# An adaLN transformer block on one core: 57 of 108 quad products moved to GpSimd in four pieces each, 3+3 quad buffers, two-bank exponential groups to the end

## The chip, the cores and the metric

The kernel runs on one core of one Trainium2 chip. The engines are TensorE (PE, with its weight loads shown as PEld), VectorE (DVE), ScalarE (ACT), GpSimd (POOL) and SyncE (SP), which issues the DMAs. The metric is the device time of one execution in microseconds. Before the change it is 815.04 us, the median of 3 runs from 815.03 to 815.05 us.

## The reference

One block over 2048 rows of 640 columns, 32 heads of 20 columns, in bf16. Only `A_x` is used as input; `B_x` is not.

```
mod = (silu(c) @ w_mod).reshape(1, 6, 1, 640)
sa, ca, ga, sb, cb, gb = mod[:, 0..5]
h = layernorm(x) * (1 + ca) + sa
q, k, v = split(h @ wqkv)                       # 32 heads of 20
o = softmax(q @ k.T / sqrt(20)) @ v             # per head, 2048 x 2048 scores
x = x + ga * (o @ wo)
h = layernorm(x) * (1 + cb) + sb
x = x + gb * (((h @ w_gate) * (h @ w_up)) @ w_down)    # F = 1536
```

The scores are 32 x 2048 x 2048 values, and each needs an exponential. That is the bulk of the elementwise work.

## The kernel before

**A planner in the builder.** The kernel file holds a small scheduler (`Sched`): every instruction is a `Task` with an engine, a planned duration, dependencies and a priority. The scheduler runs through planned time and fixes, for each engine, the order of its instructions. `emit_program` writes these orders out as five instruction streams with semaphore waits. So the chip runs a fixed order on each engine, in which every instruction waits for what it needs.

**Units of attention.** Queries go through in five chunks of 512, 512, 512, 256 and 256 rows (`CHUNKS`). An item is one chunk with four heads; there are 8 items in a chunk, 40 in all. The scores of an item are cut into units of 128 keys-partitions x 512 columns: 64 units in an item of a 512-row chunk, 32 in one of a 256-row chunk, 2048 in all. PE computes a unit's scores into one PSUM bank. The scores are scaled so that they count in 1/128 of a power of two.

**Two ways to the exponential.** Most units go to ScalarE: a group of two units (banks 0 and 1 or 3 and 4), or of three (banks 0 to 2), is exponentiated by one ACTIVATE (line 1484) into a slot of a ring `PP`, four slots for even groups and four for odd ones. From group 580 on (`HEADG`) even groups have three banks; up to there bank 2 serves as a third bank of the pool `G`, which holds projections, FFN results and quads' scores. The other units go to VectorE, four at a time; four such units are a quad (`QUADS` gives the number of quads of each item). A quad costs:

- four evacuations P1 (line 1508): PSUM bank to an int16 buffer `DB`, 128x512 each;
- two splits of that buffer, 128x2048 int16: M (line 1540, the mantissa, into a slot of `DSS`) and EX (line 1548, the exponent, into another slot);
- one product X (line 1545): `DB` times the mantissa term, 128x2048 bf16, in place in the slot of M.

Both terms are then multiplied with the values, so a quad's units pass through the value matmuls (line 2005) twice (`NTERM` = 2), a ScalarE unit once. There are `NB0` = 2 buffers `DB` and `NSS` = 3 slots `DSS`.

**Value products.** Line 2005 accumulates an item's output, with the softmax denominator in an extra value column, in the one bank 7. When all units of an item are in, VectorE transposes the bank (T1, line 1632), takes the reciprocal of the denominators, GpSimd multiplies (T3, line 1638), VectorE transposes back (T4, line 1646), and DMAs copy the heads to where the output projection reads them. The next item's value products wait for T1.

**Work beside it.** During chunk 0 PE computes the projections to queries, keys and values (lines 1107, 1171, 911). During each chunk from the second on it does the suffix of the chunk before: output projection, layer norm, gate, up and down projections (line 911 and, in the tail, 907), with evacuations on VectorE. `GATE_F` spreads these over the groups of the chunk. The suffix of the last chunk is the tail. Where PE would idle, it may run matmuls that add zeros (lines 2355 and 2357).

**PE's order.** `pick_pe` prefers a group's score step, to which up to two units of quads may be attached (`d_attach`), if their banks in `G` are free. After that come value products and then projection or FFN rounds. `STAGE` overrides the thresholds of these choices item by item.

**The shared port in the planner.** Tasks that the planner takes to use the SBUF port pair which VectorE and GpSimd share carry `lk`: splits and products on VectorE (1), most GpSimd tasks (1). `Sched.locked` keeps such a task from starting while one of the other engine runs. Pieces of a product on GpSimd carry `lk` = 2: before, they may not start either while VectorE has a port task ready. `Sched.lock` also makes such a piece wait for VectorE's last port task. With `X_POOL` = 0 no product goes to GpSimd, so no task has `lk` = 2 before the change.

Of the kernel before, what the change touches and what calls it, by code (L numbers as in the profile page):

```python
# [30 lines left out]
HAM_MIN = 2550.0  # L31

# [85 lines left out]
class Sched:  # L118
# [32 lines left out]
    def locked(self, eng, task):  # L151
        if not task.lk:
            return False
        if self.lk_end["pool" if eng == "dve" else "dve"] > self.t:
            return True
        if task.lk == 2:
            for d in self.readyl["dve"]:
                if d.lk and d.rt <= self.t and d.gate <= self.progress and (d.cond is None or d.cond()) and all(
                        a[0].avail() is not None and a[0].avail()[0] <= self.t for a in d.acq):
                    return True  # L160
        return False
# [160 lines left out]
def emit_program(nc, sched, nsem_dma=56):  # L322
# [83 lines left out]
    with nc.Block() as block:  # L406
# [20 lines left out]
        def _(e):  # L427
# [5 lines left out]
QUADS = ((0, 4, 3, 3, 3, 3, 4, 4),  # L433
         (3, 4, 2, 4, 3, 4, 4, 4),
         (3, 3, 4, 4, 3, 4, 4, 4),
         (1, 2, 1, 2, 2, 1, 1, 2),
         (1, 1, 1, 1, 1, 1, 1, 1))
D_LEAD = 0.451
NB0, NSS = 2, 3
HEADG = 580  # L440
# [7 lines left out]
X_POOL, X_PIECES, POOL_NS = 0, 4, 1.95  # L448
X_LAST = 2
X_TAIL = 0  # L450
XBACK = 1
HOLD = 110
PVTOL = 249
XDPRIO = 1.447
# [8 lines left out]
WM_GATE = 9  # L463
# [9 lines left out]
PVMIN, PVMAX, PVCAP = 2, 7, 13  # L473
# [13 lines left out]
GATE_F = (0.468, 0.693, 0.969, 0.732, 1.0)  # L487
FILL_MIN = 4153.722
# [23 lines left out]
    0: {"X_LATE": -179.96, "D_RES": 74, "EAGER": 9, "PVMAX": 14},  # L512
    1: {"HOLD": 91, "D_LATE": 10, "PVMAX": 7},
    2: {"DL": 0.376, "D_LATE": 17},
    3: {"STEAL_GAP": 200, "PVMAX": 5, "FILL_MIN": 4781.051, "X_LATE": 38.763},
    5: {"EAGER": 7, "D_RES": 27, "PVCAP": 8},
    6: {"PVCAP": 12, "FILL_MIN": 4102.43, "D_LATE": 12, "PVMIN": 2},
    7: {"DL": 0.501, "PVCAP": 8, "PVTOL": 347},
    10: {"PVMAX": 8, "X_LATE": -27.967, "EAGER": 11, "D_LATE": 9},
    11: {"EAGER": 11, "DL": 0.443, "X_LATE": -8.435, "FILL_MIN": 4364.854, "PVTOL": 245, "HOLD": 134, "PVMAX": 9, "PVCAP": 13},  # L520
    12: {"FILL_MIN": 4969.105, "D_LATE": 7, "STEAL_GAP": 194.93, "X_LATE": -138.337, "DL": 0.459},
    13: {"DL": 0.417, "D_RES": 10, "HOLD": 84, "PVMAX": 6},
    14: {"D_LATE": 14, "D_RES": 22, "FILL_MIN": 4272.896, "EAGER": 10, "X_LATE": -52.696, "STEAL_GAP": 200},
    15: {"X_LATE": -15.741, "FILL_MIN": 4338.164, "HOLD": 175, "EAGER": 13},
    16: {"FILL_MIN": 3909.78, "D_RES": 55, "HOLD": 133, "PVCAP": 11},
    17: {"DL": 0.465, "D_LATE": 17, "PVMAX": 9, "PVMIN": 2, "STEAL_GAP": 195.663},
    18: {"FILL_MIN": 4326.704, "D_RES": 10},
    19: {"D_LATE": 18, "DL": 0.471, "FILL_MIN": 3976.707},
    20: {"DL": 0.391, "D_LATE": 14, "PVCAP": 13, "FILL_MIN": 5000},
    21: {"D_RES": 10, "PVCAP": 20, "HOLD": 96, "PVMAX": 6, "PVMIN": 2, "D_LATE": 19},  # L530
    22: {"PVMAX": 7, "FILL_MIN": 3913.503, "D_RES": 17, "X_LATE": -76.434, "EAGER": 6, "D_LATE": 16, "PVCAP": 13},
    23: {"PVTOL": 247, "PVMAX": 7, "D_RES": 23},
    24: {"PVCAP": 13, "PVMAX": 7, "PVMIN": 2, "FILL_MIN": 4085.526, "DL": 0.464, "EAGER": 7, "STEAL_GAP": 200, "HOLD": 231},
    25: {"HOLD": 174, "X_LATE": 22.894, "D_RES": 13, "FILL_MIN": 4068.834, "DL": 0.608, "PVCAP": 17, "D_LATE": 14, "EAGER": 5, "Z_LATE": -10.124, "PVTOL": 224},
    26: {"D_RES": 21, "X_LATE": -37.237, "PVMAX": 9, "PVCAP": 13, "STEAL_GAP": 193.843, "DL": 0.411, "FILL_MIN": 3349.471, "D_LATE": 18},
# [1897 lines left out]
```

## Time and profile before

| what | value |
|---|---|
| median of 3 runs | 815.04 us (815.03 to 815.05) |
| the profiled execution | 815.03 us |
| its span, first to last instruction | 813.2 us |
| granted TensorE clock, mean | 1.000 |
| exponentials on ScalarE: of two banks, of three | 676, 97 in the grouped rows (774 in all) |
| first and last exponential | 16.0 us to 779.4 us |
| GpSimd's normalizing products of 128x512 (T3) | 24, mean 1526 ns; shortest 1.05 us, longest 4.85 us |
| DMA moved | 54.70 MB, mean 67 GB/s |

The span is the time between the first and the last instruction in the trace; some 1.8 us of the execution lie outside it. An instruction's duration on ScalarE and VectorE overlaps that of the next, so rates are taken from starts or from busy time. A row of the grouped view names the line, the engine, the operation, output and inputs, the count, the busy time and the mean of one, then the idle time of the engine in front of these instructions and what ended it. A row of the waits names who waited for whom: total, times, longest. A row of a stretch lists the busy time of PE, PEld, DVE, ACT and POOL in it.

### The profile page before, as it was taken

Reading aid. Unit: us, or ns where it says so; the run is one execution under the profiler, and the core shown is the slowest. Engines: PE = TensorE matmul, PEld = TensorE weight load, DVE = VectorE, ACT = ScalarE, POOL = GpSimd, SP = SyncE. Lnnn points to the kernel's source line nnn. Section 1 sums busy time; section 2 is a strip of 40 time slices with the busy share of each in tenths; the row PEclk is TensorE's granted clock in tenths of the full one; section 3 lists DMA queues with packets and bytes.
Section 4 is the critical chain, followed back from the end, with each engine's and each line's share of the span. In section 5 each row is a group of like instructions: output and inputs, shape, how many; then the busy total and the mean of one; then the engine's idle time right before and its main releaser. Section 6 shows DMA issues by size and latency. Waiting matters only on the chain.

```text
span 813.2 us, 28869 instructions
## 1 busy us (share of the span) xinstructions
PE 785.0 (97%) x12485; PEld 305.5 (38%) x12485; DVE 724.7 (89%) x1283; ACT 772.8 (95%) x816; POOL 79.4 (10%) x106
## 2 busy tenths in 40 slices
PE   9999999999999999999999999999888999999998
PEld 4433333322233223233233322333244444454567
DVE  7989999899999999999999999998999878667763
ACT  7899999999999999999999999999999999999941
POOL 3300000020002000000011000000021000001000
PEclk9999999999999999999999999999999999999999
DMA  9624211114330244000400222000400145106520
GB/s 305 210 86 106 68 46 38 50 30 126 93 67 25 52 107 130 23 11 22 93 6 6 55 54 55 6 19 23 87 8 15 45 95 129 45 22 128 126 61 17
DMA packets 116445, 54.70 MB, mean 67 GB/s; under 512 B 83916, under 2 KB 116320, under 8 KB 116320
## 3 DMA queue, kind: packets, MB, share of 16 engines
q1 hardware_dynamic: 115391, 51.72, 24.7%
q8 instruction: 99, 1.62, 0.8%
q10 hardware_dynamic: 928, 1.15, 0.4%
q14 instruction: 27, 0.21, 0.1%
HBM read 41.85 MB, written 8.41 MB: 62 GB/s over the span
## 4 chain that ended last, share of the span: by engine, by line
PE 47%; ACT 34%; DVE 12%; issue 6%; POOL 0%; DVEq 0%; ACTq 0%; POOLq 0%
ACT PP L1484 34%; PE ps_all L911 16%; PE ps_all L1448 14%; PE ps_all L2005 10%; DVE DB L1508 5%; PE ps_all L907 3%; DVE DSS L1545 2%; DVE DSS L1548 1%; DVE DSS L1540 1%; PE ps_all L1171 1%; PE ps_all L1107 1%; PE ps_all L2355 1%; PE ps_all L1068 1%; DVE wd L1434 1%; DVE OT L1632 1%
## 5 line engine op out<-in xcount | busy, mean ns | idle before, releaser
L1484 ACT ACTIVATE PP<-ps_all 128x1024 bf16<-128x1024 f32 (+1 forms) x774 | 754.2, 1168 | 5.0 <-PE ps_all L1448 3.0
L1448 PE MATMUL ps_all<-QT,KT 32*128 32x512 bf16 (+1 forms) x2560 | 308.4, 340 | 17.9 <-ACT PP L1484 11.6
L1508 DVE TENSOR_SCALAR DB<-ps_all 128x512 int16<-128x512 f32 x404 | 267.4, 680 | 33.7 <-PE ps_all L1448 32.5
L1448 PEld LDWEIGHTS ps_all<-QT,KT 32*128 32x128 bf16 x2560 | 81.5, 91 | 262.5 <-ACT PP L1484 227.6
L2005 PE MATMUL ps_all<-PP,Vf 128*32 128x512 bf16 (+2 forms) x2076 | 163.5, 343 | 0.0
L1545 DVE TENSOR_TENSOR DSS<-DB,DSS 128x2048 bf16<-128x2048 bf16 x101 | 123.6, 1223 | 0.0
L911 PE MATMUL ps_all<-h2T,stg 128*32 128x512 bf16 (+1 forms) x1744 | 116.4, 344 | 1.8 <-DVE DB L1508 1.1
L1638 POOL TENSOR_TENSOR OTn<-OT,invT 128x512 bf16<-128x512 f32 (+1 forms) x39 | 46.7, 1197 | 601.0 <-DVE invT L1636 601.0
L2005 PEld LDWEIGHTS ps_all<-PP,Vf 128*32 128x32 bf16 (+1 forms) x2076 | 46.9, 94 | 85.5 <-issue 78.7
L2005 PE MATMUL ps_all<-DSS,Vf 128*32 128x512 bf16 (+1 forms) x968 | 77.9, 348 | 0.9 <-DVE DSS L1545 0.5
L1540 DVE TENSOR_SCALAR DSS<-DB 128x2048 int16<-128x2048 int16 x101 | 71.1, 704 | 0.8
L1548 DVE TENSOR_SCALAR DSS<-DB 128x2048 int16<-128x2048 int16 x101 | 69.7, 690 | 0.3 <-PE ps_all L2005 0.3
L911 PE MATMUL ps_all<-wd,hprod 128*32 128x320 bf16 (+1 forms) x1312 | 58.9, 284 | 0.5 <-DVE xckt L1730 0.2
L911 PEld LDWEIGHTS ps_all<-h2T,stg 128*32 128x32 bf16 x1744 | 38.9, 95 | 36.6 <-issue 18.3
L911 PEld LDWEIGHTS ps_all<-wd,hprod 128*32 128x32 bf16 x1312 | 30.8, 96 | 17.9 <-issue 8.0
L2005 PEld LDWEIGHTS ps_all<-DSS,Vf 128*32 128x32 bf16 x968 | 24.3, 95 | 24.5 <-issue 15.0
L911 PE MATMUL ps_all<-wV,hT 128*32 128x320 bf16 (+1 forms) x704 | 32.3, 289 | 0.1
L1171 PE MATMUL ps_all<-hT,wq 128*32 128x512 bf16 x375 | 31.6, 382 | 0.1
L911 PE MATMUL ps_all<-wo,Ocp 128*32 128x320 bf16 (+1 forms) x632 | 28.9, 286 | 1.1 <-DVE DB L1508 0.6
L1863 DVE TENSOR_TENSOR hprod<-ps_all,gsb 128x512 bf16<-128x512 f32 x36 | 24.4, 678 | 3.3 <-PE ps_all L911 3.3
L1632 DVE STREAM_TRANSPOSE OT<-ps_all 128x512 f32<-128x512 f32 (+1 forms) x40 | 24.1, 602 | 2.5 <-PE ps_all L2005 2.3
L2357 PE MATMUL ps_all<-ident 128*32 128x512 bf16 x284 | 25.7, 384 | 0.3 <-DVE DB L1508 0.2
(125 smaller groups left out, 505.5 us busy)
## 6 DMA issues: line engine op xcount, KB each, us to landing
stg<-in_B_w_gate_dram SPq DMA_DIRECT2D x50, 160.0 KB, 2.6
stg<-in_B_w_up_dram SPq DMA_DIRECT2D x50, 160.0 KB, 2.4
QT<-q_rows SPq DMA_DIRECT2D x22, 128.0 KB, 2.0
KT<-k_rows SPq DMA_DIRECT2D x84, 32.0 KB, 1.8
wm<-in_w_mod_dram SPq DMA_DIRECT2D x3, 800.0 KB, 5.6
x<-in_A_x_dram SPq DMA_DIRECT2D x7, 320.0 KB
xck<-in_A_x_dram SPq DMA_DIRECT2D x3, 640.0 KB
wd<-in_B_w_down_dram SPq DMA_DIRECT2D x1, 1920.0 KB
```

The costliest lines, as they stand in the source:

```text
L911: return lambda e, b: e.matmul(ps[32 * x:32 * x + 32, b, c0 + o:c0 + o + w], lhs()[:, 32 * x:32 * x + 32], rhs() if w == n else rhs()[:, o ...
L1171: f = [lambda e, b_, k=k, x=x: e.matmul(ps[x:x + min(32, w - x), b_, :], wx[:, k, r0 + x:r0 + min(x + 32, w)], hT[tc][:, k, :], tile_posit ...
L1448: ems.append(lambda e, i=i, kt=kt: e.matmul(dstf()[:, i * u.n:(i + 1) * u.n], KT[32 * u.s:32 * u.s + 32, u.j, kt * 128:(kt + 1) * 128], QT ...
L1484: return e.activation(PPs[g % 2][:, cellp["p"], 0:nu * 512], ps[:, b0:b0 + nu, :].rearrange("p b c -> p (b c)"), AFT.Exp, scale=ESCALE)
L1508: return e.tensor_scalar(DB0[:, st_["slot"], x * 512:(x + 1) * 512], bank(cell["b"]), EBIAS, 0.0, op0=ALU.add, op1=ALU.max)
L1540: return e.tensor_scalar(DSS[:, st_["ss"][0], :], DB0[:, st_["slot"], :], 0x7F, 0x3F00, op0=ALU.bitwise_and, op1=ALU.bitwise_or)
L1545: return e.tensor_tensor(d, DB0[:, st_["slot"], :].bitcast(BF16), d, ALU.mult)
L1548: return e.tensor_scalar(DSS[:, st_["ss"][1], :], DB0[:, st_["slot"], :], 0x7F80, 2, op0=ALU.bitwise_and, op1=ALU.bitwise_or)
L1632: t1 = Task("dve", n * 1.1 + 70, lambda e: e.transpose(OT[:, 0:n], ps[:, BPV, 0:n].rearrange("p (b q r) -> p b r q", q=32, r=2)), [], prio ...
L1638: f3 = lambda e: e.tensor_tensor(OTn[:, 0:n].rearrange("p (b c r) -> p b r c", c=32, r=2), OT[:, 0:n].rearrange("p (b r c) -> p b r c", c= ...
L2005: ems.append(lambda e, i=i, kt=kt, stt=stt, stp=stp: e.matmul(ps[32 * s:32 * s + mc, BPV, 0:u.n], Vf[:, (kt * H + 4 * u.j + s) * VW:(kt * ...
L2357: task.emits = [lambda e, x=x: e.matmul(ps[32 * x:32 * x + 32, b_, :].rearrange("p (a b) -> p a b", a=4), ident[:, 32 * x:32 * x + 32], id ...
```

## The change

It has six parts.

1. **Products on GpSimd.** `X_POOL` = 1: each quad's product except the last quad's may be done by VectorE as one 128x2048 operation, or by GpSimd as four operations of 128x512 (`X_PIECES`), whichever the planner starts first. In the plan 57 of 108 products go to GpSimd and 51 to VectorE. A piece waits for M and for EX of its quad. The splits get priority 0.75, ahead of P1 (0.8); VectorE's product gets 1.343.
2. **When a piece may start.** With `LKTOL` a piece may start although VectorE has a port task ready, if VectorE's work ahead of that task lasts until at most 300 ns before the piece's end in the plan.
3. **Quads.** 108 in place of 101: per chunk 25, 29, 30, 12, 12 in place of 24, 28, 29, 12, 8. ScalarE's units fall from 1644 to 1616. Which units of an item form its quads is generalized, so that an item may have more quads than one diagonal of heads and key tiles gives.
4. **Buffers.** Three `DB` buffers in place of two, three `DSS` slots as before.
5. **Two-bank groups to the end.** `HEADG` = 1000 is past the last group, so no group has three banks, bank 2 stays with `G`, and all slots of the ring have two banks (which frees the memory of the third `DB` buffer).
6. **Choices of the planner.** New thresholds for each item (`STAGE`), new gates, `WM_GATE` 8 in place of 9 (a load of modulation weights may start one group earlier), and in the tail a projection round that is blocked may be overtaken by any round of higher priority. `XB0`, `XSS` and what uses them are 0 and do nothing.

```diff
-            for d in self.readyl["dve"]:
-                if d.lk and d.rt <= self.t and d.gate <= self.progress and (d.cond is None or d.cond()) and all(
+            tt = max(self.t, self.free_at["dve"])
+            for d in sorted(self.readyl["dve"], key=lambda x: (x.prio, x.seq)):
+                if d.rt <= self.t and d.gate <= self.progress and (d.cond is None or d.cond()) and all(
                         a[0].avail() is not None and a[0].avail()[0] <= self.t for a in d.acq):
-                    return True
+                    if d.lk:
+                        return tt < self.t + task.dur - LKTOL
+                    tt += d.dur
...
-QUADS = ((0, 4, 3, 3, 3, 3, 4, 4),
-         (3, 4, 2, 4, 3, 4, 4, 4),
-         (3, 3, 4, 4, 3, 4, 4, 4),
+QUADS = ((0, 4, 3, 3, 3, 4, 4, 4),
+         (3, 5, 2, 4, 3, 4, 4, 4),
+         (4, 2, 4, 4, 4, 4, 4, 4),
          (1, 2, 1, 2, 2, 1, 1, 2),
-         (1, 1, 1, 1, 1, 1, 1, 1))
+         (0, 2, 1, 1, 3, 0, 3, 2))
-NB0, NSS = 2, 3
-HEADG = 580
+NB0, NSS = 3, 3
+XB0, XSS = 0, 0
+HEADG = 1000
-X_POOL, X_PIECES, POOL_NS = 0, 4, 1.95
-X_LAST = 2
+X_POOL, X_PIECES, POOL_NS = 1, 4, 1.95
+X_LAST = 1
-XBACK = 1
+XBACK = 0
-XDPRIO = 1.447
+XDPRIO = 1.343
-WM_GATE = 9
+WM_GATE = 8
-PVMIN, PVMAX, PVCAP = 2, 7, 13
+PVMIN, PVMAX, PVCAP = 2, 7, 12
-GATE_F = (0.468, 0.693, 0.969, 0.732, 1.0)
-FILL_MIN = 4153.722
+GATE_F = (0.446, 0.693, 0.969, 0.658, 1.0)
+FILL_MIN = 4190.746
...
-                q = kg // 4
-                u.is_d = q < nq and s == kg % 4
+                x4 = nkg // 4
+                q = kg // 4 + x4 * ((s - kg) % 4)
+                u.is_d = q < nq
...
-        for q in quads:
+        for q in sorted(quads, key=lambda q: (q[0].kts[0] // (4 * rr), q[0].s)):
             dquads.append((it, q))
...
-                    if blocked and task.name[:3] != "col":
+                    if blocked and task.name[:3] != "col" and not (pvstate["sidx"] >= NG and task.prio < cand.prio):
                         continue
```

The task of a piece was in the file before and is now reached:

```
t = Task("pool", w * POOL_NS + 180.0, fxp, [tm, te], prio=2.0 + .1 * qi + .01 * x, name=f"XP.{qi}")
t.lk = 2
```

## The prediction

> **What bounds the kernel now.** I read the engine totals first, then ScalarE's waits, then the starts of the exponentials, then busy time by stage.
>
> ```profile
> PE 785.0 (97%) x12485; PEld 305.5 (38%) x12485; DVE 724.7 (89%) x1283; ACT 772.8 (95%) x816; POOL 79.4 (10%) x106
> ```
>
> Three engines are near full and GpSimd is nearly empty, so totals don't name the bound. ScalarE's waits do:
>
> ```profile
> ACT h2Tc L1770 <- PE ps_all L1763: 9.9, 1, 9.9
> ACT gsb L1826 <- PE ps_all L907: 9.3, 12, 1.4
> ACT PP L1484 <- PE ps_all L1448: 3.0, 6, 1.3
> ```
>
> The two large waits lie behind the last exponential (779.4 us). In front of it the exponentials run from 16.0 us almost without a gap; the timeline of ScalarE shows 0.7 us of idle after 61 us. So up to 779.4 us the end is set by the number of units on ScalarE times its price. The starts in three stretches of 100 us (count, durations, first and last start):
>
> ```profile
> L1484 ACT ACTIVATE PP<-ps_all x110: 1017/1132/1252, 99.3 to 199.1; 128x1024 bf16<-128x1024 f32 x110
> L1484 ACT ACTIVATE PP<-ps_all x111: 1019/1154/1323, 199.1 to 300.0; 128x1024 bf16<-128x1024 f32 x111
> L1484 ACT ACTIVATE PP<-ps_all x89: 1017/1451/1613, 649.4 to 749.9; 128x1536 bf16<-128x1536 f32 x45, 128x1024 bf16<-128x1024 f32 x44
> ```
>
> A two-bank group comes every 99.8/109 to 100.9/110, about 0.919 us over the stretches of this stage, so 0.4595 us for a unit of 512 columns. A pair of a three-bank and a two-bank group takes 2 x 100.5/88 = 2.284 us for five units, 0.4568 us for a unit. Durations overlap, so I count starts and not means. The other engines by stage (PE, weight loads, DVE, ACT, POOL):
>
> ```profile
> 260.00:360.00 100.00, 99.30 (x1371) 31.08 (x1374) 97.28 (x159) 99.90 (x109) 6.19 (x5) 1.00 0.25 65
> 320.00:560.00 240.00, 234.33 (x3407) 77.20 (x3404) 235.75 (x380) 239.43 (x261) 19.37 (x18) 1.00 0.14 33
> 680.00:740.00 60.00, 57.59 (x1322) 29.19 (x1314) 43.27 (x80) 59.69 (x53) 4.84 (x7) 1.00 0.26 63
> 779.40:813.20 33.80, 30.59 (x425) 24.52 (x420) 16.18 (x44) 5.53 (x15) 1.10 (x2) 0.99 0.07 23
> ```
>
> From 320 to 560 us DVE is 98% full: no further quad fits there. Late (680 to 740 us) DVE is 72% full, but PE 96%. The tail of 33.8 us is PE's.
>
> **Exponentials removed.** Seven more quads take 28 of 1644 units off ScalarE: 28 x 0.4595 = 12.9 us less. Four quads are in the last chunk, three in the first three.
>
> **Three-bank groups given up.** 484 units ran in pairs of 3+2; as two-bank groups each costs 0.4595 - 0.4568 = 0.0027 us more: 1.3 us (0 by the pair at 600 to 700 us, which took 0.459 a unit). I take 1.3.
>
> **Products moved.** The rows, with count, busy time and mean of one:
>
> ```profile
> L1508 DVE TENSOR_SCALAR DB<-ps_all 128x512 int16<-128x512 f32 x404 | 267.4, 680 | 33.7 <-PE ps_all L1448 32.5
> L1545 DVE TENSOR_TENSOR DSS<-DB,DSS 128x2048 bf16<-128x2048 bf16 x101 | 123.6, 1223 | 0.0
> L1540 DVE TENSOR_SCALAR DSS<-DB 128x2048 int16<-128x2048 int16 x101 | 71.1, 704 | 0.8
> L1548 DVE TENSOR_SCALAR DSS<-DB 128x2048 int16<-128x2048 int16 x101 | 69.7, 690 | 0.3 <-PE ps_all L2005 0.3
> ```
>
> DVE does 108 - 57 = 51 products in place of 101: 50 x 1.223 = 61.2 us less. The seven quads add 28 x 0.662 (267.4/404) = 18.5 and 14 x 0.697 = 9.8 us. DVE goes from 724.7 to about 692 us. GpSimd gets 57 x 4 = 228 pieces of 128x512. No such piece is in the trace; the nearest row is its normalizing product on 128x512 f32, 1.05 us where nothing holds it up, 0.62 us on 256 columns, so a piece is bounded by 0.62 below and by the worst such row, 4.85 us, above. I take 1.05: the same columns, two inputs. That is 239 us on an engine that has 734 us free, off the path by itself. By the Trainium skill (GPSIMD Engine Reference, Performance versus the Vector engine), elementwise work belongs on VectorE, since GpSimd's tensor_tensor on 2048 fp32 elements takes 4497 ns; by that 57 products would be an estimated 256 us, which changes the load and not the bound.
>
> **The price is the lock.** What a piece blocks is shown around 176 us, first GpSimd, then DVE:
>
> ```profile
> 175.93 4.85 POOL L1638 TENSOR_TENSOR OTn<-OT,invT 128x512 bf16<-128x512 f32 x1 [20.39 <-DVE invT L1636]
> ```
>
> ```profile
> 175.78 0.62 DVE L1548 TENSOR_SCALAR DSS<-DB 128x2048 int16<-128x2048 int16 x1
> 176.32 1.20 DVE L1545 TENSOR_TENSOR DSS<-DB,DSS 128x2048 bf16<-128x2048 bf16 x1
> 177.45 0.68 DVE L1540 TENSOR_SCALAR DSS<-DB 128x2048 int16<-128x2048 int16 x1
> 178.06 0.68 DVE L1548 TENSOR_SCALAR DSS<-DB 128x2048 int16<-128x2048 int16 x1
> 178.66 1.21 DVE L1545 TENSOR_TENSOR DSS<-DB,DSS 128x2048 bf16<-128x2048 bf16 x1
> ```
>
> GpSimd's 1.05 us became 4.85: it ended 1 us after the fifth DVE operation on SBUF. The other way round, at 542.16 us a split (L1540) took 1.54 in place of 0.68 us, since a GpSimd product had started at 541.24. The PSUM evacuations (L1508) beside such products keep their length (0.69 us at 126.57). So splits and products on DVE and pieces on GpSimd exclude each other, evacuations don't. From 320 to 560 us: 39 quads before, about 40 after, 53% of them on GpSimd, 85 pieces. DVE would hold 235.8 - 0.53 x 39 x 1.227 (47.84 us busy in that window, by 39) + 1.3 x 4.6 (one quad without its product) = 216 us in about 237. The slack of 21 us is 0.25 us for each piece. The port itself: pieces 89, other GpSimd work 19, splits 56 and products 23 us, together 187 of 237, so it fits if ordered. The builder lets a piece start only where DVE has other work for all but 0.3 us of it, and DVE's order is fixed with that in view; I take a mean stall of about 0.15 us a piece, inside the slack. Behind a stalled split on DVE stand the evacuations, behind them the score banks, behind these the next exponential: I give 1 us of ScalarE waits (0 to the rival's price below). Three buffers of each kind hold a quad for the longer product; they add nothing by themselves, and the cover for a late product is the ring of eight probability slots, about 7 us of exponentials.
>
> **PE late.** Two-bank groups need more score steps: each takes 0.33 us of PE to the start of the next work and about 0.12 of switching (at 709.11 us two steps of 320 columns, 0.27 us of streaming, and the next score step starts 0.39 us on), 2.5 units a step before and 2 after. What that leaves for projections and FFN I work out from the columns of their matmuls by stage, at 0.217 us for a step of four matmuls of 512 columns side by side (20 of them at 12.96 us take 1.25 us, one alone 0.38: 0.87/4). At two banks with PE full that is 32.5 us in the 100 us from 260 us, and 31.8 us from 460 us. From 600 to 779.4 us PE placed 24.2 + 22.2 + 14.1 = 60.5 us of it. The same window will be 179.4 - 16 x 0.4595 + 1.2 = 173.2 us long. At 33% (the fuller stage, and half a point for a quad share of 12 in 64 instead of 29 in 128, whose second value products PE is spared) it holds 57.2, so 3.3 us move behind the last exponential, where PE is busy 30.6 of 33.8 us. I take 3.3; with PE's idle of now (4%, 7 us) it is 10, and none if the third evacuation bank cures the idle of that stage (8.5 us). The extra value products of the seven quads are inside the measured share. Earlier weight loads by one group, new gates and the pre-emption rule at the end add no instruction or DMA; the last can move at most PE's 3.2 us of tail idle. I count them at 0.
>
> **Sum.** Span 813.2 - 12.9 + 1.3 + 1.0 + 3.3 = 805.9. The profiled execution took 815.03 us, 1.83 outside its span, and the median is 815.04, so 807.7 us.
>
> **Rivals.** (1) PE becomes the bound after 600 us: 10 us of backlog in place of 3.3, and 1 to 2 us of score waits: about 815 us, no change. For it: PE is continuous from 752 to 778 us in the chain. Against: fills and idle of 11 us in that stage. (2) The port makes DVE the bound, and the kernel is slower. Place: 80 to 560 us. Point: a mean stall above 0.25 us a piece. At 0.33 us the excess is 0.08 x 228 = 18 us less what the late stage's spare DVE hides (a fifth): 801.6 + 14.4 + 1.0 + 3.3 + 1.8 = 822 us. For it: a hit costs 0.86 us (1.54 against 0.68), so 38% of pieces hitting is enough. Against: 70% of DVE's time is evacuation that isn't blocked, and pieces are a quarter of a product, so a hit is short. The Trainium skill (SBUF — State Buffer, Who interferes with whom) states this as an exclusive lock that goes to whichever starts first for the whole instruction; the trace agrees (4.85 and 1.54 us). (3) The late stage hides all of it, with idle of PE cured: 813.2 - 12.9 + 1.3 = 801.6 + 1.8 = 803.4, perhaps 801 with the tail rule. (4) It doesn't do what it says: GpSimd starves behind chains like the one at 176 us, the ring runs dry at item ends and ScalarE waits 3 us at each of some 6 items: 807.7 + 18 = 826.
>
> **Chances.** Forecast 0.50 (its own range 803 to 812), rival 1 0.18, rival 2 0.18, rival 3 0.10, rival 4 0.04. A measurement can tell about 0.2%, 1.6 us, from no change, so faster is below 813.4. Faster: 0.50 + 0.10 + 0.06 of rival 1 = 0.66; within: 0.08 of rival 1; slower: 0.04 + 0.18 + 0.04 = 0.26. The range of 800 to 820 leaves out most of rivals 2 and 4 and the far end of 3.
>
> **What would show it.** 808 two-bank exponentials at 0.92 us and the last one at about 769 us. DVE busy near 692 us plus stalls, seen as splits longer than 0.70 us; a mean above 0.95 would mean rival 2. GpSimd near 320 us, pieces near 1.05 us; longer ones would show starving. PE: projections and FFN behind the last exponential above 34 us mean rival 1. ScalarE idle between 61 us and the last exponential above 5 us would make the forecast wrong.

## The result, and the profile after

The changed kernel takes 811.88 us (median of 20 runs, 810.54 to 815.70) beside 815.03 us for the kernel before on the same chip (20 runs, 814.94 to 815.48). The ratio is 0.9963, with a 95% interval of 0.9955 to 0.9971: faster by 0.37%, 3.2 us. The forecast was 807.7 us, 7.3 us faster. The profiled execution is the shortest of the 20, 1.3 us below the median, so the profile below shows a span that is 4.3 us shorter and not 3.2.

The engine totals of the changed kernel (busy time, share of the span, instructions):

```profile
PE 792.8 (98%) x12585; PEld 303.3 (37%) x12585; DVE 703.1 (87%) x1273; ACT 764.0 (94%) x853; POOL 321.2 (40%) x330
```

Its span is 808.9 us beside 813.2, and the profiled execution took 810.54 us beside 815.03. ScalarE, VectorE and GpSimd moved as the change says. TensorE has 7.8 us more than before (785.0), although the profile counts only 100 matmuls more (12585 in place of 12485). The groups behind these totals (count, busy time and mean duration, then the idle time ahead of them and what ended it):

```profile
L1497 ACT ACTIVATE PP<-ps_all 128x1024 bf16<-128x1024 f32 x808 | 744.1, 1143 | 5.3 <-PE ps_all L1461 4.4
L1573 POOL TENSOR_TENSOR DSS<-DB,DSS 128x512 bf16<-128x512 bf16 x224 | 254.9, 1156 | 324.6 <-DVE DSS L1561 235.9
L1561 DVE TENSOR_SCALAR DSS<-DB 128x2048 int16<-128x2048 int16 x108 | 75.9, 703 | 0.0
L1553 DVE TENSOR_SCALAR DSS<-DB 128x2048 int16<-128x2048 int16 x108 | 75.5, 699 | 0.5
L1558 DVE TENSOR_TENSOR DSS<-DB,DSS 128x2048 bf16<-128x2048 bf16 x52 | 67.2, 1292 | 0.2
```

808 exponentials, all of two banks; 224 pieces on GpSimd, which is 56 products and not the 57 that were named ahead of the run, and 52 on VectorE. The splits cost 0.70 us, as before. ScalarE's waits from 61 us to its last exponential (time, times, longest):

```profile
ACT PP L1497 <- PE ps_all L1461: 2.6, 5, 0.9
```

The last exponential ends at 770.19 us; before it was 779.44. So ScalarE finished 9.25 us earlier, but the kernel only 4.3: what lies behind it grew from 33.8 to 38.7 us. TensorE's side shows why. The windows of the late stage and of the tail (PE, weight loads, VectorE, ScalarE, GpSimd, then TensorE's clock, DMA share, GB/s):

```profile
600.00:700.00 100.00, 99.49 (x1908) 41.20 (x1900) 77.93 (x140) 99.94 (x109) 36.91 (x39) 1.00 0.28 65
700.00:770.20 70.20, 70.10 (x1638) 36.72 (x1640) 57.14 (x116) 69.76 (x76) 31.78 (x33) 1.00 0.36 82
770.20:808.90 38.70, 34.91 (x538) 27.65 (x527) 20.30 (x50) 6.23 (x16) 3.16 (x4) 1.00 0.16 43
```

TensorE is busy 169.6 of 170.2 us from 600 us up to the last exponential; 4.0 us of that are the matmuls that add zeros (L2382). The same windows of the kernel before:

```profile
600.00:700.00 100.00, 95.32 (x1916) 43.34 (x1912) 84.46 (x149) 99.47 (x89) 9.50 (x15) 1.00 0.28 65
700.00:779.40 79.40, 75.56 (x1859) 41.57 (x1851) 54.97 (x109) 79.31 (x70) 6.25 (x10) 1.00 0.38 84
779.44:813.20 33.76, 30.55 (x425) 24.48 (x417) 16.18 (x44) 5.49 (x14) 1.10 (x2) 0.99 0.07 23
```

There TensorE had 8.5 us of idle ahead of the last exponential, and 2.8 us of zero matmuls. Now it has 0.6 us of idle. The chain of work that ended last points the same way: ScalarE's share of it falls from 34% to 24%, TensorE's rises from 47% to 63%. Two engines are full at once in this stage, and which of them sets the pace can't be read from busy time; that is what the experiments are for.

**Where the gain accrues.** Each of the 40 items of attention ends with one transpose of its output (L1632 before, L1645 after), so their starts show how far ahead the changed kernel is. Read off the timelines of VectorE, in us (single items scatter by some us, since the order inside an item differs: item 31 is 10.3 us ahead, item 32 only 2.0):

```
item              4       12       22       30       36       39
before       151.45   334.81   561.83   669.07   742.24   780.25
after        149.59   331.48   556.69   663.75   737.44   775.17
difference    -1.86    -3.33    -5.14    -5.32    -4.80    -5.08
```

Items 0 to 23 hold three of the seven added quads, 12 units, 5.5 us by the prediction's price, and gain 5.1 us. Items 24 to 31 have the quads that they had. Items 32 to 39 hold the other four quads, 16 units or 7.4 us, and gain nothing. With that scatter the table is a hint; experiments 5 and 7 test it. Behind the last transpose 33.73 us follow in place of 32.95, which takes 0.8 back: -5.1 + 0.8 = -4.3, the difference of the two spans.

### The profile page after: what moved, and what is told of

Its sections match the earlier page's. It is cut to its first block, busy times and chain, and to the rows that moved or that the text cites. A ratio compares the mean times of both kernels' runs of the same rounds, so it can differ in the third digit from the quotient of the medians.

```text
span 808.9 us, 29314 instructions
## 1 busy us (share of the span) xinstructions
PE 792.8 (98%) x12585; PEld 303.3 (37%) x12585; DVE 703.1 (87%) x1273; ACT 764.0 (94%) x853; POOL 321.2 (40%) x330
## 4 chain that ended last, share of the span: by engine, by line
PE 63%; ACT 24%; DVE 9%; issue 4%; SPq 0%; DMA 0%; POOL 0%; ACTq 0%; DVEq 0%; POOLq 0%
ACT PP L1497 23%; PE ps_all L1461 21%; PE ps_all L923 17%; PE ps_all L2018 14%; PE ps_all L1183 4%; DVE DB L1521 3%; PE ps_all L919 3%; PE ps_all L1119 1%; PE ps_all L2382 1%; PE ps_all L2380 1%; DVE DSS L1561 1%; DVE DSS L1558 1%; DVE DSS L1553 1%; PE ps_all L1080 1%; DVE st L1757 0%
## 5 line engine op out<-in xcount | busy, mean ns | idle before, releaser
L1497 ACT ACTIVATE PP<-ps_all 128x1024 bf16<-128x1024 f32 x808 | 744.1, 1143 | 5.3 <-PE ps_all L1461 4.4
L1573 POOL TENSOR_TENSOR DSS<-DB,DSS 128x512 bf16<-128x512 bf16 x224 | 254.9, 1156 | 324.6 <-DVE DSS L1561 235.9
L1521 DVE TENSOR_SCALAR DB<-ps_all 128x512 int16<-128x512 f32 x432 | 288.6, 684 | 44.0 <-PE ps_all L1461 41.6
L2018 PE MATMUL ps_all<-PP,Vf 128*32 128x512 bf16 (+1 forms) x2032 | 158.8, 343 | 0.3 <-DVE OT L1645 0.3
L2018 PE MATMUL ps_all<-DSS,Vf 128*32 128x512 bf16 (+2 forms) x1056 | 84.4, 343 | 0.4 <-POOL DSS L1573 0.2
L1561 DVE TENSOR_SCALAR DSS<-DB 128x2048 int16<-128x2048 int16 x108 | 75.9, 703 | 0.0
L1553 DVE TENSOR_SCALAR DSS<-DB 128x2048 int16<-128x2048 int16 x108 | 75.5, 699 | 0.5
L2018 PEld LDWEIGHTS ps_all<-PP,Vf 128*32 128x32 bf16 x2032 | 44.7, 94 | 78.2 <-issue 72.1
L1558 DVE TENSOR_TENSOR DSS<-DB,DSS 128x2048 bf16<-128x2048 bf16 x52 | 67.2, 1292 | 0.2
L2018 PEld LDWEIGHTS ps_all<-DSS,Vf 128*32 128x32 bf16 (+1 forms) x1056 | 26.4, 95 | 19.8 <-issue 7.7
L1865 DVE CAST gsb<-ps_all 128x512 bf16<-128x512 f32 x36 | 24.5, 681 | 8.3 <-PE ps_all L923 8.2
L1645 DVE STREAM_TRANSPOSE OT<-ps_all 128x512 f32<-128x512 f32 (+1 forms) x40 | 24.2, 604 | 7.5 <-PE ps_all L2018 7.5
```

Source lines behind the costliest of these rows:

```text
L1497: return e.activation(PPs[g % 2][:, cellp["p"], 0:nu * 512], ps[:, b0:b0 + nu, :].rearrange("p b c -> p (b c)"), AFT.Exp, scale=ESCALE)
L1521: return e.tensor_scalar(DBl[st_["slot"]][:, x * 512:(x + 1) * 512], bank(cell["b"]), EBIAS, 0.0, op0=ALU.add, op1=ALU.max)
L1553: return e.tensor_scalar(DSl[st_["ss"][0]][:, :], DBl[st_["slot"]][:, :], 0x7F, 0x3F00, op0=ALU.bitwise_and, op1=ALU.bitwise_or)
L1558: return e.tensor_tensor(d, DBl[st_["slot"]][:, :].bitcast(BF16), d, ALU.mult)
L1561: return e.tensor_scalar(DSl[st_["ss"][1]][:, :], DBl[st_["slot"]][:, :], 0x7F80, 2, op0=ALU.bitwise_and, op1=ALU.bitwise_or)
L1573: return e.tensor_tensor(d, DBl[st_["slot"]][:, x * w:x * w + w].bitcast(BF16), d, ALU.mult)
```

## The experiments

Times are medians, with the range of the runs; the kernel before took 815.0 us beside each of them. The spread of the changed kernel needs a word first.

**1. The changed kernel once more.** No edit.

> The changed kernel once more, unchanged, for a second profile and the spread of its times. Theory A (a race for the shared port costs a varying amount in mid-stream): times spread over 3 us or more again, and a profile of a slower execution shows the loss as ScalarE idle of 1 to 5 us between 60 us and the last exponential, with the tail behind the last exponential within 0.5 us of 38.7. Theory B (the variation is in the tail, where the last quads wait for port and DMA): ScalarE's idle in mid-stream stays within 0.5 us of 1.8 us and the tail moves by as much as the total.

Measured: 810.83 us (810.42 to 811.84, 5 runs), ratio 0.995 (0.9938 to 0.9963). On this chip the gain is 4.2 us. The item transposes agree with those of the first profile to 0.03 us until item 36, so here both executions differ only in the last 70 us. The five runs spread over 1.4 us, less than the first theory asks, and two profiles of almost equal times can't test the second. The kernel before varies by 0.5 us over its 20 runs, the changed one by 5: five of its 20 runs took more than 813 us. None of these was profiled, and what lengthens them stays open.

**2. The port.** Pieces of 8 columns in place of 512 (the product is left out but for 32 of 2048 columns of a quad):

```diff
-d = DSl[st_["ss"][0]][:, x * w:x * w + w].bitcast(BF16)
-return e.tensor_tensor(d, DBl[st_["slot"]][:, x * w:x * w + w].bitcast(BF16), d, ALU.mult)
+d = DSl[st_["ss"][0]][:, x * w:x * w + 8].bitcast(BF16)
+return e.tensor_tensor(d, DBl[st_["slot"]][:, x * w:x * w + 8].bitcast(BF16), d, ALU.mult)
```

> The changed kernel with each GpSimd piece cut to 8 of its 512 columns (the other columns keep the mantissa term, so the attention output differs); same order on every engine. It takes the port's price away, and the product's length with it. Theory A (the port costs little in the middle, the loss sits in the tail and in the price of a unit): time falls by 1 to 3 us, of which over half in the tail, and the spread of the runs shrinks below 1 us. Rival (stalls on the port hold the score banks and ScalarE): the last exponential comes 4 us or more earlier than 770.2 us and the total falls by 5 us or more.

Measured: 811.30 us (810.71 to 811.59), ratio 0.9954, beside 810.83 us for the changed kernel on the same chip: no gain, where I had expected 1 to 3 us. The same rows, for this kernel:

```profile
L1573 POOL TENSOR_TENSOR DSS<-DB,DSS 128x8 bf16<-128x8 bf16 x224 | 40.8, 200 | 470.7 <-DVE DSS L1561 339.0
L1561 DVE TENSOR_SCALAR DSS<-DB 128x2048 int16<-128x2048 int16 x108 | 75.0, 694 | 0.0
L1553 DVE TENSOR_SCALAR DSS<-DB 128x2048 int16<-128x2048 int16 x108 | 73.9, 685 | 0.7 <-PE ps_all L2018 0.2
L1558 DVE TENSOR_TENSOR DSS<-DB,DSS 128x2048 bf16<-128x2048 bf16 x52 | 63.2, 1214 | 0.2
```

All that the pieces cost VectorE is the difference of the three DVE rows: 0.9 + 1.6 + 4.0 = 6.5 us, 0.03 us a piece, and ScalarE's waits are the same 2.6 us. So the port costs little in this order: rival 2 is dead, and so is the 1.0 us that I had put on stalls.

**3. What GpSimd's share is worth.** The changed kernel with all products on VectorE again:

```diff
-X_POOL, X_PIECES, POOL_NS = 1, 4, 1.95
+X_POOL, X_PIECES, POOL_NS = 0, 4, 1.95
```

> The changed kernel with all 108 products on VectorE (no piece on GpSimd), its other choices as they are; the planner orders the work anew. Theory A (the quads are paid for by VectorE time that the moved products free, and the port is free of charge): VectorE goes back to 98% full between 80 and 560 us, evacuations come late and ScalarE waits for scores there; 820 to 830 us. Rival (the move brings nothing, VectorE had room): within 2 us of the changed kernel.

Measured: 825.33 us (824.95 to 825.60), ratio 1.0126 (1.0113 to 1.0139). VectorE is at 751.2 us, and from 61 us to the last exponential ScalarE waits at

```profile
ACT PP L1497 <- PE ps_all L2018: 9.1, 3, 6.8
ACT PP L1497 <- PE ps_all L1461: 2.4, 8, 0.7
```

The first of these is ScalarE without a free probability slot, behind a late product: at the longest wait VectorE ends a product at 272.27 us, the item's last value matmuls follow at 272.38, those of the next item, which free a slot, at 273.68, and ScalarE goes on at 274.11. So with these thresholds 108 quads can't be had without GpSimd. They were tuned for GpSimd's share, so the 13 to 14 us beside the changed kernel are an upper bound of what the share is worth.

**4. Two-bank groups alone.** The kernel before with the groups of the changed kernel:

```diff
-HEADG = 580
+HEADG = 1000
```

> The kernel before with two-bank groups to the end and nothing else changed (101 quads, all products on VectorE). It prices the giving up of three-bank groups. By the terms of the prediction: 1.3 us for ScalarE, and up to 1 us of PE backlog, since this late stage is 7 us longer than the changed kernel's: 816 to 818 us. Rival (PE is the bound late, each further score step is paid in full): 48 more groups of 0.45 us less 11 us of fills and idle, 825 us.

Measured: 820.34 us (820.21 to 820.73), ratio 1.0067 (1.0054 to 1.0081): 5.3 us slower, where I had reckoned with 1.3 to 2.3 and the rival with 10. The thresholds were not refitted to it. It has 822 exponential groups in place of 774 (first the kernel before, then with two banks):

```profile
L1484 ACT ACTIVATE PP<-ps_all 128x1024 bf16<-128x1024 f32 (+1 forms) x774 | 754.2, 1168 | 5.0 <-PE ps_all L1448 3.0
L1484 ACT ACTIVATE PP<-ps_all 128x1024 bf16<-128x1024 f32 x822 | 757.0, 1125 | 4.5 <-PE ps_all L1448 3.0
```

Score matmuls of the last two chunks, by shape, in the kernel before, with two banks, and in the changed kernel:

```profile
L1448 PE MATMUL ps_all<-QT,KT 32*128 32x256 bf16 x1024 | 73.6, 272 | 7.4 <-ACT PP L1484 4.0 <-DVE DB L1508 2.2 <-DVE hprodt L1832 0.4
```

```profile
L1448 PE MATMUL ps_all<-QT,KT 32*128 32x256 bf16 x1024 | 86.8, 273 | 2.5 <-ACT PP L1484 2.3
```

```profile
L1461 PE MATMUL ps_all<-QT,KT 32*128 32x256 bf16 x1024 | 83.9, 273 | 1.7 <-ACT PP L1497 1.6
```

The same 1024 matmuls, as long each, keep TensorE busy 13.2 us longer with two banks. The 432 units of these chunks then come in 216 groups in place of some 173, so that is 0.3 us for each group more; in the changed kernel it is 10.3 us for some 35 groups more. Part of it fills idle time: that in front of these matmuls falls from 7.4 to 2.5 us (1.7 in the changed kernel). Busy time is the union of matmuls that overlap: 1024 x 0.273 = 280 us of them fit into 73.6 us, 3.8 at once, with three banks, and 3.2 at once with two. All of it falls in the late stage; items 0 to 21 end where they did to 0.05 us. On ScalarE the step costs 757.0 - 754.2 = 2.8 us. Item 39 ends 2.2 us later than in the kernel before, and what follows the last exponential is 3.0 us longer.

**5. Is the late stage TensorE's? In the changed kernel.** The last 22% of the exponentials compute half of their columns; every engine keeps its order.

```diff
+w = 256 if g >= int(0.78 * NG) else 512
-return e.activation(PPs[g % 2][:, cellp["p"], 0:nu * 512],
-                    ps[:, b0:b0 + nu, :].rearrange("p b c -> p (b c)"), AFT.Exp, scale=ESCALE)
+return e.activation(PPs[g % 2][:, cellp["p"], 0:nu * w],
+                    ps[:, b0:b0 + nu, :].rearrange("p b c -> p (b c)")[:, 0:nu * w], AFT.Exp, scale=ESCALE)
```

> The changed kernel with the last 22% of the exponential groups (178 of 808) computing only half of their columns, so that each takes about 0.5 instead of 0.92 us; the other half of the weights is left as it was in the buffer. Nothing else changes, TensorE has the same matmuls in the same order, and ScalarE gets some 75 us of room from about 600 us on. Theory (from 600 us on TensorE is as full as ScalarE: 169.6 of 170.2 us busy): the time falls by less than 1.5 us, to 809.5 or more beside 811 for the changed kernel. Rival (ScalarE alone sets the late stage, and TensorE's busy time is stretched by waiting): it falls by 4 us or more.

Measured: 811.42 us (810.34 to 812.24), ratio 0.9955 (0.9942 to 0.9969), no change beside 811.88 and 810.83. ScalarE got 59 us of room (705.2 us busy in place of 764.0), and spent it waiting for scores (waits of all engines from 600 to 771 us, the largest of ScalarE's):

```profile
ACT PP L1498 <- PE ps_all L1461: 58.3, 171, 0.8
```

The windows of the late stage, in the order of columns as above:

```profile
600.00:700.00 100.00, 99.42 (x1910) 41.44 (x1914) 78.11 (x140) 66.22 (x109) 37.47 (x40) 1.00 0.28 65
700.00:770.07 70.07, 70.07 (x1632) 36.38 (x1628) 56.96 (x115) 45.05 (x76) 31.17 (x32) 1.00 0.35 81
```

171 groups of 178 wait for TensorE, and TensorE is busy as long as before to 0.1 us in each window. From 600 us on it sets the pace in this order, and its busy time isn't stretched by waiting for ScalarE.

**6. The same in the kernel before.**

> The kernel before with the same cut (the last 22% of its 774 exponential groups compute half of their columns). TensorE is busy 170.9 of 179.4 us from 600 us to the last exponential there. Theory (TensorE's matmuls are a floor under the late stage, at which the changed kernel has arrived): the time falls by 4 to 8 us, to 807 to 811, that is to within 2.5 us of the changed kernel with the same cut. Rival (no such floor): it falls by about as much as the changed kernel does under the cut, and stays 3 to 4 us above it.

Measured: 813.43 us (813.36 to 815.74), ratio 0.9986 (0.9977 to 0.9995). I had expected 807 to 811: the theory of a floor holds, but I had thought that most of the 8.5 us of idle on TensorE could be filled. They can't, they are waits of their own. TensorE's waits from 600 to 770 us, with the cut:

```profile
PE ps_all L911 <- DVE DB L1509: 2.9, 7, 0.7
PE ps_all L1448 <- DVE DB L1509: 1.7, 3, 0.7
...
PE ps_all L1448 <- ACT PP L1485: 0.3, 1, 0.3
```

and without it:

```profile
PE ps_all L911 <- DVE DB L1508: 2.5, 6, 0.6
PE ps_all L1448 <- ACT PP L1484: 2.1, 7, 0.7
PE ps_all L1448 <- DVE DB L1508: 1.4, 2, 0.7
```

Only the 2.1 us of waits for ScalarE could be had; 1.6 us came out. The larger part is TensorE waiting for VectorE to empty the quads' score banks (DB). So already in the kernel before, with its order kept, the late stage was not ScalarE's: half of its exponentials could be dropped for a gain of 1.6 us.

**7. The last chunk's quads put back.** In the changed kernel:

```diff
-         (0, 2, 1, 1, 3, 0, 3, 2))
+         (1, 1, 1, 1, 1, 1, 1, 1))
```

> The changed kernel with the last chunk's quads as in the kernel before: eight in place of twelve, one an item. 16 units go back to ScalarE, all of them after 590 us, eight exponentials more (816), which is 16 x 0.4595 = 7.4 us of ScalarE. In the kernel before and the changed kernel the transposes that end the items (L1632 before, L1645 after) come 5.1 us earlier after the change at item 22 (556.69 beside 561.83 us) and still 5.1 us earlier at the last item (775.17 beside 780.25 us). Theory (in the last chunk TensorE sets the pace, and units taken off ScalarE there bring nothing): the time rises by less than 3 us over the 811 to 812 of the changed kernel, that is to 815 at most. Rival (ScalarE sets the pace there too): it rises by about 7 us, to 818 or 819.

Measured: 813.20 us (812.62 to 814.33, 11 runs), ratio 0.9977 (0.9968 to 0.9986). 16 units more on ScalarE (751.6 us of exponentials in place of 744.1) cost 1.3 to 2.4 us beside the changed kernel's 811.88 and 810.83, not 7. The last exponential does end 8.8 us later, at 779.0 us, but only 33.2 us follow it in the profile (span 812.2) in place of 38.7: what ScalarE loses in front of its last exponential, TensorE's backlog behind it gives back. The thresholds were not refitted to these quads.

```profile
L1497 ACT ACTIVATE PP<-ps_all 128x1024 bf16<-128x1024 f32 x816 | 751.6, 1145 | 6.4 <-PE ps_all L1461 5.6
```

**8. Three-bank groups back, late quads left out.** If two-bank groups eat late what the four late quads bring, then a kernel with neither is as fast. The changed kernel with three-bank groups from group 608 on, eight quads in the last chunk, and the thresholds and gates of the planner refitted (some of the edit):

```diff
-HEADG = 1000
+HEADG = 608
-         (0, 2, 1, 1, 3, 0, 3, 2))
+         (0, 0, 2, 1, 1, 2, 1, 1))
-    wo7 = alloc("wo7", [128, D], BF16)
+    wo7 = at("wo7", [128, D], BF16, late_off + FT * D * 2)
-    KPB = alloc("KPB", [128, 2, 512], BF16)
+    KPB = at("KPB", [128, 2, 512], BF16, late_off)
```

> The changed kernel with three-bank groups from group 608 on, as the kernel before has them from 580 on, with eight quads in the last chunk in place of twelve (104 in all), and the planner's thresholds fitted to that. To make room for the longer probability slots beside three DB buffers, two tiles (KPB, and the seventh row block of wo) share memory that is free at their time. ScalarE has 1632 units in place of 1616, in 775 exponentials. GpSimd's share stays. Theory (in the last chunk TensorE sets the pace, and two-bank groups cost it some 10 us there, about what the four late quads were meant to bring): the score matmuls of 256 columns take 76 us or less of TensorE in place of 83.9, the last exponential ends some 5 us later than in the changed kernel, at about 775 to 776 us, and the time is that of the changed kernel or up to 1.5 us below, 809.5 to 812. Rival (ScalarE sets the pace to the end): 16 units more cost 7 us, 817 us or more.

> The changed kernel without an edit, on the same chip as the run with three-bank groups, for the comparison. Its other runs had medians of 811.88 and 810.83 us; 810.4 to 812.5 is expected by every theory.

Measured: 810.96 us (810.55 to 811.22, 5 runs), ratio 0.9950 (0.9936 to 0.9963), beside 811.57 us (810.94 to 812.05, 5 runs), ratio 0.9957 (0.9944 to 0.9969), for the changed kernel on the same chip. Its totals, exponentials, score matmuls and late windows:

```profile
PE 785.0 (97%) x12449; PEld 301.9 (37%) x12449; DVE 679.1 (84%) x1239; ACT 768.9 (95%) x818; POOL 354.6 (44%) x362
L1497 ACT ACTIVATE PP<-ps_all 128x1024 bf16<-128x1024 f32 (+1 forms) x775 | 749.8, 1173 | 5.6 <-PE ps_all L1461 4.5
```

```profile
L1461 PE MATMUL ps_all<-QT,KT 32*128 32x256 bf16 x1024 | 74.2, 273 | 5.7 <-ACT PP L1497 3.9 <-DVE DB L1521 1.1 <-DVE gsb L1865 0.2
```

```profile
700.00:776.00 76.00, 71.90 (x1762) 39.84 (x1758) 51.99 (x110) 75.45 (x67) 36.64 (x38) 1.00 0.40 86
776.00:809.20 33.20, 29.87 (x378) 23.56 (x370) 15.84 (x42) 5.63 (x15) 1.10 (x2) 0.99 0.06 21
```

The 7.8 us that TensorE was busy longer are gone, and so is the long tail: the last exponential ends at 776.1 us, 5.9 later than in the changed kernel, and 33.1 us follow it in place of 38.7. 16 units more on ScalarE cost nothing, where ScalarE's price is 7.4 us (749.8 us of exponentials in place of 744.1, since three-bank groups cost less a unit). The new thresholds also put 64 of the 104 products on GpSimd in place of 56, and the four quads fewer spare TensorE value matmuls, so the run shows that leaving out both costs nothing, and not the price of each. The 0.6 us by which its median is lower are not told apart from nothing (the intervals overlap); its runs spread over 0.7 us.

**9. The tail.** Three runs asked what sets the 5 us by which the tail is longer, and the spread. In the changed kernel the end of TensorE's timeline reads

```profile
772.46 0.84 PE L923 MATMUL ps_all<-h2Tt,stg 128*32 128x256 bf16 x24 [0.45 <-DMA stg<-in_B_w_up_dram]
773.26 0.63 PE L2018 MATMUL ps_all<-DSS,Vf 128*32 128x256 bf16 x16
773.71 0.62 PE L923 MATMUL ps_all<-h2Tt,stg 128*32 128x256 bf16 x16
774.50 0.41 PE L2018 MATMUL ps_all<-DSS,Vf 128*32 128x256 bf16 x8 [0.17 <-POOL DSS L1573]
775.28 2.08 PE L919 MATMUL ps_all<-wo,Ocp 128*128 128x320 bf16 x14 [0.38 <-DMA Ocp<-OcT]
```

(start, duration). The last value products come 3 to 4 us after the last exponential, behind FFN matmuls that were pushed past it, and the output projection waits for the copies of the next-to-last item's output.

First, the products of the last two quads cut to 8 columns, so that no late piece can hold up a value product:

```diff
-d = DSl[st_["ss"][0]][:, :].bitcast(BF16)
+c_ = 8 if qi >= len(dquads) - 2 else 2048
+d = DSl[st_["ss"][0]][:, 0:c_].bitcast(BF16)
...
-d = DSl[st_["ss"][0]][:, x * w:x * w + w].bitcast(BF16)
+c_ = 8 if qi >= len(dquads) - 2 else w
+d = DSl[st_["ss"][0]][:, x * w:x * w + c_].bitcast(BF16)
```

> The changed kernel with the products of the last two quads alone cut to 8 columns (four pieces on GpSimd, one product on VectorE; output of the last item differs); same order everywhere. Theory A (the last quads' chain, split at 770.4 us, product, last piece behind the product until 774.4 us, sets the start of the tail): the last output transpose moves from 5.0 us behind the last exponential to about 3 us behind it, and the total falls by 1 to 2 us. Rival (PE's backlog of projections sets the tail): the total falls by less than 0.5 us, and PE stays over 90% busy between the last exponential and the end.

Measured: 811.45 us (810.70 to 812.29), ratio 0.9958. The last transpose still comes 4.8 us after the last exponential: the quads' chain isn't what is late.

Second, the weight loads of the FFN of the chunk before the last cut to a fifth (its gate and up projections use what was in the buffer):

```diff
+if ci == 3:
+    return e.dma_start(cell["t"][:, 0:1, :], wv[:, 0:1, fc * 128:(fc + 1) * 128])
```

> The changed kernel with the loads of chunk 3's gate and up weights cut to a fifth of their rows (the rest keeps the older weights; its output differs). Before the change no PE step in the tail waited for such a load; after it one does (0.45 us at 772.5 us, in front of the last value products). Theory A (the larger spread of the times comes from that load's landing): the spread of five runs falls below 0.5 us from 1.4 us and the total by 0.5 us. Rival (the spread comes from elsewhere): spread of 1 us or more as before, total within 0.3 us.

Measured: 811.25 us (810.64 to 811.70), ratio 0.9953. The wait for these loads is gone and the projection waits for the copies instead, 1.3 us, until 776.43. Nothing is gained, and the five runs spread over 1.1 us, where the theory asked for less than 0.5.

Third, two of the five copies issued by ScalarE:

```diff
+for t in sched.all:
+    if t.name in ("O38.1", "O38.3"):
+        t.eng = "act"
```

> The changed kernel with one thing moved: of the five copies that carry the next-to-last item's normalized output from OcT into Ocp, two are issued by ScalarE right behind the last exponential instead of by SP (all engines keep the order they had). In the changed kernel SP issues the five in a row from 770.37 to 774.11 us, and in five profiled executions the first matmul of the last output projection started between 775.17 and 776.43 us, in four of them after 0.4 to 1.6 us of waiting for these copies. Theory (the landing of these copies starts the tail): with three on SP the last is issued by about 772.6, the projection starts at about 774.9 us without a wait on them, and the time is 810.0 to 810.8 in nearly all runs, a median some 1.0 us below the 811.88 of the changed kernel and a spread under 1 us. Rival (the spread comes from other transfers, such as the weight loads of the last gate and up projections): the median stays within 0.4 us of 811.5 and the spread stays over 1.2 us.

Measured: 810.72 us (810.28 to 811.87), ratio 0.9949 (0.9936 to 0.9961). The profiled execution took 811.87 us, the longest of the five, and lost 1.5 us between its items 1 and 2, long before the tail. In it the projection no longer waits for the copies:

```profile
776.00 0.41 PE L2021 MATMUL ps_all<-DSS,Vf 128*32 128x256 bf16 x8
776.61 2.06 PE L922 MATMUL ps_all<-wo,Ocp 128*128 128x320 bf16 x14 [0.20 <-issue]
```

The other four runs took 810.28 to 810.88 us. This fits the theory, but five runs don't tell it from the 810.83 of the changed kernel on another chip, and transfers earlier than the tail vary too. That the copies start the tail in some runs is shown by the waits of 0.4 to 1.6 us; what makes up the whole of the spread stays open.

**10. Less work for TensorE late.** The gate and up projections of the chunk before the last were cut to 32 of 256 columns, in the changed kernel and in the kernel before, to see how much of the late stage is their work.

```diff
+w = min(w, cut or w)
...
+**({"cut": 32} if ci == 3 else {})
```

> The changed kernel with the gate and up matmuls of chunk 3's suffix cut to 32 of 256 columns (its output differs), orders unchanged: it takes up to 11 us of PE's late work away. Theory A (after the change PE is the bound in the last 200 us: 99.6% busy, and what it can't place stands in front of the last value products): the last output transpose comes earlier, the tail falls from 38.6 to 35 us or less and the total by 3 to 6 us. Rival (a chain of waits behind the last exponential, on DMA and on the last quads, sets the tail): the total falls by less than 1.5 us.

> The same cut in the kernel before, as a control. There PE was 96% busy late and its leftover matmuls lay beside the chain from the last value product to the last layer norm. Theory A: the total falls by less than 1.5 us, under half of what it does for the changed kernel. Rival (PE was the bound late already): it falls as much as there, 3 us or more.

Measured: 816.8 us (814.38 to 818.96) after and 818.36 us (815.71 to 818.71) before. Both are slower with less work, and the granted clock fell in both. The windows with the cut, three of the changed kernel and then one of the kernel before:

```profile
720.00:740.00 20.00, 19.90 (x433) 9.67 (x430) 18.20 (x37) 19.97 (x23) 10.77 (x12) 1.00 0.49 114
740.00:760.00 20.00, 18.91 (x448) 9.22 (x444) 15.70 (x33) 18.70 (x20) 7.37 (x7) 0.64 0.40 89
760.00:780.00 20.00, 15.98 (x463) 8.79 (x460) 18.17 (x35) 13.24 (x16) 7.41 (x7) 0.67 0.33 73
760.00:780.00 20.00, 19.25 (x490) 9.77 (x482) 14.30 (x27) 19.15 (x18) 0.62 (x1) 0.50 0.46 105
```

The clock (the third figure from the end) goes from 1.00 to 0.64 and 0.67, and to 0.50 in the kernel before. The pair says nothing on the question, and experiments 5 and 6, which leave TensorE's work alone, took its place.

## Why the prediction was wrong, and what of it held

- **What bounds the kernel: the step that failed.** I read "up to 779.4 us the end is set by the number of units on ScalarE times its price" from its timeline, 0.7 us of idle after 61 us. An engine without idle is a bound only if no other engine has as little room, and the prediction's own row for 680 to 740 us has TensorE busy 57.6 of 60 us. Up to 590 us ScalarE as the bound fits: 12 units were put at 5.5 us, and 5.1 came, with 2.2 us of waits of ScalarE; no run shrank the early exponentials, so this half rests on the agreement. After that it was not so: half of the late exponentials can go for 1.6 us before the change and for nothing after it.
- **Exponentials removed, -12.9 us.** The size on ScalarE was right: 757.0 us with two banks (experiment 4) and 744.1 in the changed kernel is 12.9 us. But 7.4 of them, 16 units, were taken off in the last chunk, where they brought little: item 39 is as far ahead as item 22, 5.1 us, and experiment 7 puts them at 1.3 to 2.4 us. For the kernel as changed this term should have been -5.5, or -7 to -8 with what experiment 7 gives. In the terms of the sum as it stands, the last exponential came 9.3 us earlier where 10.6 were forecast, and 4.9 us moved behind it where 3.3 were: that makes 4.3 us in place of 7.3. The median's gain is smaller still, 3.2 us, because of the spread of the changed kernel, which stays open.
- **PE late, +3.3 us.** The mechanism was the right one, and it was mis-sized and used wrongly: I let ScalarE's whole gain pass and added a backlog behind it, where TensorE's full late stage was a floor under it. The backlog was 4.9 us, and with three-bank groups (experiment 8) it is gone.
- **Three-bank groups given up, +1.3 us.** I priced the step on ScalarE alone, from the starts of its groups. It is 2.8 us there, and it keeps TensorE busy 10 to 13 us longer, 5 to 8 of them beyond the idle that it fills, in the stage where TensorE is the floor. By itself it costs the kernel before 5.3 us, and in the changed kernel it takes about what the four late quads bring (experiment 8).
- **Products moved, and the lock, +1.0 us.** Right in direction: VectorE at 703 us (692 plus stalls forecast), GpSimd at 321 (320), with 224 pieces and not 228. A piece takes 1.156 us and not 1.05. Stalls are 0.03 us a piece, 6.5 us in all, where I took 0.15, 34 us in all; they cost the kernel nothing. By the Trainium skill (SBUF — State Buffer, Who interferes with whom) the pair of ports is held by one engine at a time. The trace agrees with it only in how little is left to see: all 224 pieces lie between 1.146 and 1.167 us, so none was cut into by VectorE, since the plan starts a piece only where VectorE has other work.
- **The rivals.** Rival 1, TensorE as the bound after 600 us, is what happened; I gave it 0.18 and 815 us. Its price was too high: 4.9 us of backlog came in place of 10, and 0.4 us of score waits after 600 us in place of 1 to 2. Rivals 2 and 4 are refuted by experiment 2 and by ScalarE's 2.6 us of waits. Rival 3, in which the idle of TensorE late is cured, was half true: the idle went from 8.5 to 0.6 us, but the score matmuls of the two-bank groups keep TensorE busy 10.3 us longer.
- **What would show it.** I had named the tail above 34 us as the sign of rival 1, and it shows: 38.7 us. 808 exponentials and the last one at 770 us, beside 769 forecast, came out as well, and mislead if read alone.

## What to carry to other kernels

An engine without idle time is the bound only where no other engine is as full: price a saving stage by stage, and count it only where the second-fullest engine has the room for it. A cheap test is to shrink the suspected engine's instructions late in the kernel and to leave everybody's order alone; if the end stays, the saving has no one to go to. A change of grouping is to be priced on every engine that handles the groups, not only on the one whose overhead it was made for.

## What the runs showed of the hardware

- The same matmuls hold TensorE longer when they are issued in smaller groups between other work: 1024 score matmuls of 256 columns took 73.6 us in groups of three and two banks and 86.8 us in groups of two in the kernel before; in the changed kernel they took 83.9 us, and 74.2 us with three-bank groups.
- Less matmul work can be slower. With the columns of some late matmuls cut from 256 to 32 the granted clock fell from 1.00 to 0.64 (0.50 over 760 to 780 us in the kernel before), and the kernels lost 3 to 5 us. The Trainium skill (TensorE: Matmul & The Clock Gate, Part 1) has the clock follow how busy the array has lately been; the trace agrees, in that less work per matmul brought the clock down, though the instructions still fill 95% of the stretch at 0.64; no run here shows which measure of the work counts.
- GpSimd on bf16 with two inputs: 1.156 us for 128x512 and 0.200 us for 128x8, alike to 1% over 224 pieces when VectorE stays off the port.
